# Attention and channel mixing on one core: a planned order of operations replaced by an order read from a table

## Chip, cores and metric

One core of a Trainium2 chip. The metric is the device time of one execution in microseconds (us). Engines: PE (matrix products, with PEld for its weight loads), DVE (vector engine), ACT (scalar engine), POOL (GpSimd), and SP, whose queue issues the DMAs.

## What is computed

Four batches, 8 heads, 768 tokens, head size 64, all in fp32. Attention is local, with 24 block summaries beside the near keys:

```python
k_sum = k.reshape(B, H, nb, 32, D).max(axis=3)
v_sum = v.reshape(B, H, nb, 32, D).mean(axis=3)
mask_l = np.abs(pos[:, None] - pos[None, :]) < 16
scores_s = scale * (q · k_sum) + np.log(32)
a = softmax(concat(where(mask_l, scale * q @ k.T, -1e9), scores_s))   # divided by sum + 1e-9
x = a @ concat(v, v_sum)                     # heads side by side: (4, 768, 512)
xk = mu_k * x + (1 - mu_k) * x_prev          # x_prev: the token before
xr = mu_r * x + (1 - mu_r) * x_prev
out = sigmoid(xr @ w_r) * (maximum(xk @ w_k, 0)**2 @ w_v)   # 512 -> 1024 -> 512
```

## The kernel before

**Tiling.** Two heads make a pair (128 partitions), 768 tokens two halves of 384. A *unit* is one batch, pair and half, 32 in all. For each: a score product (24 narrow products into two PSUM tiles, L511); per head and window of 128 rows a masked minimum on DVE (L525) and an exp on ACT that also sums (L529), six of each; epsilon added to the six sums (ACT, L533) and the reciprocal (DVE, L535); six multiplications by it, one per head and window of 128x120 (POOL L540 or ACT L545); two transposes on PE (L557), each copied out by ACT (L564); the values product (24 narrow products, L577), copied out by DVE (L591) or ACT (L593). There is one PSUM tile for transposes, one for values, two for scores, and four shared by all wide products.

**Wide work per batch and half.** Tokens are mixed with their predecessors (L651/L654 and L658), split into a rounded and a remaining part (L661 and L663; in one case on PE by diagonal matrices made at L314: L680, L684, L686). Each product then takes three terms: gate products (L703 to L705, 128x512), then a sigmoid (L719); expert products in eight steps *j*, a first one (L735, 12 of 128x384), its relu, square, cast and remainder (L740, L742, L744/L745, L746), and a second one (L757, L783). Three results per half are multiplied (L789) and stored (L793).

**Weights** come as 64-bit words and are put together before use: scaling (ACT L346, POOL L349), signs (L354), two joins on DVE (L358, L362), a cast (ACT L371, POOL L373) and the remainder (DVE L385). Keys are reduced to block maxima (L437 to L445) and copied between the keys (L449); in batch 0 the block means of v are made on PE (L461, L469) and spread to the windows (L475, DVE or POOL); in later batches they come from a transposed v (L406) and small DMAs.

**The order.** No loop order is kept: every operation becomes an `Op` with its engine, buffers, length (`LENGTH`) and alternatives on other engines. `schedule` counts due times backwards from fixed ones (`GATES`, `PERIOD`, `STEP`), shifted per group by `NUDGE`, and plays a list scheduler forwards; the sequence that it finds is the sequence in which instructions are emitted, for each engine's queue and for SP's DMAs. From batch 1 on, `chain` ties PE work of three units into one operation:

```python
parts.append(units[i].scores())
parts.append(units[i - 2].values())
parts.append(units[i - 1].turn(0))          # first transpose
group({1: "score", 2: "scoreT", 3: "chain"}[len(parts)] ..., min(due), *parts)
```

Until the first gate product, PE is kept at work with products of a zero tile (`still`, L849), as many as fit into the planned gaps.

Of the kernel before, what the change touches and what calls it, by code (L numbers as in the profile page):

```python
# [18 lines left out]
DM, DF = 512, 1024  # L19
# [18 lines left out]

LENGTH = dict(
    score=865, transpose=335, vtrans=200, vpool=900, vsel=240, spread=560, spread_p=830, values=1040, scoreT=1130, chain=1975, valuesT=1290, mixe=1400, minus=200, diag=290, wminus=1250, wevac=520, none=0, gate=2790, gate_p=2100, e1=2110,  # L40
    e2a=1400, e2b=700, e2=700, e2h=350, resulth=340,
    kred=860, kred2=460, kmax=90, kcopy=225, vred=865, mask=203, rc=110, evac=470, mixd=530, sub=472, psub=480, khv=276,
    result=605, wsign=575, eps=110, wor=605, wsub=605, tiny=60, wsign_d=335,
    exp=378, pts=362, vm=165, mixa=512, cast=405, relu=375, square=413, sigmoid=494, wscale=562, wcast=510,
    norm=340, norm_d=191, norm_a=285, mixa_d=329, wscale_p=575, wcast_p=575, mixa_p=575, kcopy_p=400, evac_a=362,
)
PORT = ("wor", "wsub", "mixd", "sub", "khv", "kcopy", "spread", "wsign_d", "norm_d", "mixa_d")
TAIL = dict(PE=60, DVE=85, ACT=100, POOL=30, SP=0)
LATENCY = dict(PE=230, DVE=130, ACT=150, POOL=150, SP=0)
DMA_NS_PER_BYTE = 1 / 390.0  # L50
DMA_FIXED = 2000
GATES = (36000, 62000)
PERIOD = 52000
STEP = 4800
SLACK = 400
WARM = 230
MIX_PE = ((0, 0, 1),)
SUB_PE = ()
TABLE = 1300

NUDGE = dict(
    chain10=-6500, chain11=47000, chain13=-2000, chain14=-3500, chain15=20500, chain16=8500, chain17=11500,
    chain18=-18500, chain19=17500, chain20=1500, chain21=26500, chain22=1500, chain23=-1000, chain24=-54000,
    chain25=-27000, chain26=10000, chain27=36500, chain28=-17500, chain30=1000, chain31=15500, chain32=-33000,
    chain33=-1500, chain35=-6000, chain36=6000, chain37=42500, chain38=26000, chain39=35000, e000=1500,
    e002=500, e003=2000, e004=2000, e005=-39500, e006=-27500, e007=9000, e010=-2500, e012=-7000, e013=-29000,
    e017=45000, e100=2500, e101=4500, e102=-60000, e103=-1000, e105=-500, e106=-5000, e107=60000, e110=-500,
    e112=-7000, e113=-1500, e116=-1000, e117=3000, e200=7500, e201=-26000, e202=4000, e204=500, e206=1000,
    e207=32500, e210=-60000, e211=-1500, e212=-9500, e213=-1000, e214=4500, e216=3500, e217=1500, e300=-46000,
    e301=-30500, e302=-23500, e303=500, e304=-1000, e306=2500, e307=1000, e310=-60000, e311=-34000, e312=-27000,  # L70
    e313=2000, e314=-1500, e316=-1000, e317=500, f000=-46500, f001=-5500, f003=-13500, f005=-10500, f006=22000,
    f007=20000, f010=3500, f011=18500, f012=-14000, f013=-14500, f014=-25500, f015=-8500, f016=-4000, f100=1500,
    f101=-2500, f103=-2500, f104=2500, f105=10000, f106=-3000, f107=19500, f110=6000, f111=9000, f112=20000,
    f113=13500, f114=-14500, f115=8500, f116=10000, f117=-500, f200=13000, f203=-500, f204=-8000, f205=-34000,
    f207=-12500, f211=-2000, f212=-9000, f213=-33500, f214=20500, f215=-3000, f216=10000, f217=-7000,
    f300=-24500, f302=-26000, f303=1500, f304=1500, f307=-9500, f310=-12000, f311=-19000, f312=2000, f313=-500,
    f314=-2500, f316=-500, gate00=9000, gate01=-3500, gate10=-60000, gate11=56000, gate20=16000, gate21=60000,
    gate30=2500, gate31=60000, means1=-24500, means2=-10500, mix000=-2000, mix001=3500, mix010=1000,
    mix011=14500, mix100=-10500, mix101=-32000, mix110=20500, mix111=-39500, mix200=-21500, mix201=-21500,
    mix210=8500, mix211=-32500, mix301=27500, mix310=11000, mix311=17000, set00=2000, set01=1500, set02=7000,  # L80
    set03=-41500, set10=-6000, set11=-7500, set12=2500, set20=-1500, set22=15000, set23=-10500, set31=-59500,
    set32=-44500, unit000=500, unit001=4000, unit010=1500, unit011=2000, unit020=-9500, unit021=17000,
    unit030=2500, unit031=-60000, unit100=-4000, unit101=-19500, unit111=-3500, unit120=-3500, unit121=-33000,
    unit130=-60000, unit131=-60000, unit200=-2500, unit201=1500, unit210=-18000, unit211=19000, unit220=-3000,
    unit221=26000, unit230=2000, unit231=4500, unit300=7000, unit301=-25500, unit310=-15000, unit311=-49500,
    unit320=-12000, unit321=-2000, unit330=4500, unit331=-10500, wk0=-8500, wk1=-7500, wk3=12500, wk4=-26500,
    wk5=-60000, wk6=-56000, wk7=-9500, wr0=500, wr1=-1500, wr3=-2500, wv0=2500, wv1=2000, wv2=-35500, wv4=-500,
    wv5=1500, wv6=-44000,
)
COLD = 10000  # L90
WR = 0, 6000
EARLY = 15000
FIRST = 5000
SECOND = 5000
UNITS = 6000
BETWEEN = 5, 6, 7
LOOSE = ("mm",)
NORM = ('ACT',)
MIXA = "POOL", "DVE"
FIRST_UNITS = [(hf, p) for hf in range(2) for p in range(NPAIR)]  # L100


class Buf:


    def __init__(self, pool, n):
        self.pool, self.n, self.users, self.left, self.t = pool, n, [], 0, None


class Op:  # L110
    def __init__(self, n, ways, due, bufs, size):
        self.n, self.ways, self.due, self.bufs, self.size = n, ways, due, bufs, size
        self.deps, self.succ, self.start, self.finish, self.eng = set(), [], None, None, None


class Plan:
    def __init__(self, pools):
        self.pools, self.ops, self.count = pools, [], {p: 0 for p in pools}
        self.writers, self.readers, self.tag = {}, {}, None
# [6 lines left out]
    def op(self, eng, cost, due, emit, reads=(), writes=(), size=0, other=None):  # L126

# [4 lines left out]
        ways, kinds = {eng: (LENGTH.get(cost, 0), emit)}, {eng: cost}  # L132
        for e, kind, way in ([other] if isinstance(other, tuple) else other or []):
            ways[e] = LENGTH[kind], way
            kinds[e] = kind
        o = Op(len(self.ops), ways, due, bufs, size)
        o.tag, o.kinds = self.tag, kinds
# [14 lines left out]
        o.name = cost  # L152
        return o

    def schedule(self):

        for o in self.ops:
            for d in o.deps:
                d.succ.append(o)
            for x in o.bufs:  # L160
                x.left += 1

        for o in reversed(self.ops):
            own = 1.0e9 if o.due is None else o.due
            wait = DMA_FIXED + o.size * DMA_NS_PER_BYTE if "SP" in o.ways else min(c for c, _ in o.ways.values()) + SLACK
            o.due = min([own] + [s.due - wait for s in o.succ])
        for o in self.ops:
            o.due += NUDGE.get(o.tag, 0)
        waiting = {o: len(o.deps) for o in self.ops}
        free_slots = {p: [(0, t) for t in ts] for p, ts in self.pools.items()}  # L170
        turn = {p: 0 for p in self.pools}
        table = None
        engines = {e: 0 for e in ("PE", "DVE", "ACT", "POOL", "SP")}
        ready = {e: [] for e in engines}
        dma = 0
        order = []
        port, holder = 0, None

        def locks(o, e):
            return e == "POOL" and o.kinds[e] not in ("tiny", "none") or e == "DVE" and o.kinds[e] in PORT  # L180

        def begin(o, e, at):
            at = max(at, engines[e])
            return max(at, port) if locks(o, e) and holder != e else at

        def released(o):
            for e in o.ways:
                at = max((d.finish + (0 if d.eng == e and e != "SP" else LATENCY[d.eng]) for d in o.deps), default=0)
                ready[e].append((o, at))

        for o in self.ops:
            if not waiting[o]:
                released(o)
        while any(ready.values()):
            best = None
            for e, now in engines.items():
                pick = None
                for o, at in ready[e]:
                    start, need, ok = max(at, now, o.due - EARLY if e == "SP" else 0), {}, True
                    for x in o.bufs:  # L200
# [7 lines left out]
                    if not ok:  # L208
                        continue
# [19 lines left out]
            if e == "PE" and start < COLD:  # L229
                o.cost *= 1.6  # L230
# [712 lines left out]
```

## Time and profile before

| | us |
|---|---|
| median of 3 runs (lowest, highest) | 455.13 (454.95, 456.5) |
| profiled execution | 454.91 |
| its span, first to last instruction | 453.1 |
| PE busy in the span | 444.6 (98%) |
| PEld | 379.4 (84%) |
| ACT | 304.3 (67%) |
| DVE | 273.4 (60%) |
| POOL | 59.2 (13%) |

The profiled execution's time holds 1.8 us outside its span. PE's clock is granted in full over the span as the profile's stages show it. "Busy" for PE counts modelled ends of pipelined products, so steps from start to start tell more of PE than its busy time.

### The profile page before, as it was taken

Reading aid. Unit: us, or ns where it says so; the run is one execution under the profiler, and the core shown is the slowest. Engines: PE = TensorE matmul, PEld = TensorE weight load, DVE = VectorE, ACT = ScalarE, POOL = GpSimd, SP = SyncE. Lnnn points to the kernel's source line nnn. Section 1 sums busy time; section 2 is a strip of 40 time slices with the busy share of each in tenths; the row PEclk is TensorE's granted clock in tenths of the full one; section 3 lists DMA queues with packets and bytes.
Section 4 is the critical chain, followed back from the end, with each engine's and each line's share of the span. In section 5 each row is a group of like instructions: output and inputs, shape, how many; then the busy total and the mean of one; then the engine's idle time right before and its main releaser. Section 6 shows DMA issues by size and latency. Waiting matters only on the chain.

```text
span 453.1 us, 9740 instructions
## 1 busy us (share of the span) xinstructions
PE 444.6 (98%) x3602; PEld 379.4 (84%) x3602; DVE 273.4 (60%) x876; ACT 304.3 (67%) x923; POOL 59.2 (13%) x137
## 2 busy tenths in 40 slices
PE   9998999999999999999999999999999999999996
PEld 8866788878988888888888788888888888889885
DVE  5999999997445696465345749474434473433212
ACT  3899999998986756786777735796767644332210
POOL 0472222202110110011111000110201000000000
PEclk9999999999999999999999999999999999999999
DMA  8973668846100074520700047632400010001001
GB/s 310 391 279 129 222 210 279 260 130 204 43 1 2 27 257 153 160 99 34 222 1 1 0 172 274 218 98 60 129 1 1 1 69 1 1 2 69 1 0 69
DMA packets 27446, 51.96 MB, mean 115 GB/s; under 512 B 2951, under 2 KB 15111, under 8 KB 27399
## 3 DMA queue, kind: packets, MB, share of 16 engines
q1 hardware_dynamic: 27399, 51.35, 33.5%
q8 instruction: 28, 0.46, 0.4%
q14 instruction: 19, 0.16, 0.1%
HBM read 43.28 MB, written 6.29 MB: 109 GB/s over the span
## 4 chain that ended last, share of the span: by engine, by line
PE 85%; ACT 6%; DVE 5%; issue 1%; DMA 1%; POOL 0%; DVEq 0%; POOLq 0%
PE mm L735 27%; PE mm L757 23%; PE av L577 5%; PE sc L511 5%; PE pt L557 5%; PE mm L703 4%; PE mm L704 4%; PE mm L705 4%; PE mm L783 3%; PE av L849 3%; ACT y L529 2%; ACT y L545 1%; DMA st<-in_w_k 1%; PE mm L680 1%; DVE wc L362 1%
## 5 line engine op out<-in xcount | busy, mean ns | idle before, releaser
L735 PE MATMUL mm<-xs,wk_h 128*128 128x384 f32 x512 | 101.2, 339 | 0.5 <-ACT r L740 0.3
L735 PEld LDWEIGHTS mm<-xs,wk_h 128*128 128x128 f32 x512 | 90.2, 188 | 5.7 <-ACT r L740 0.7
L529 ACT ACTIVATE y<-y,mn 128x120 f32<-128x120 f32 x192 | 73.5, 386 | 2.8 <-DVE mn L525 2.7
L740 ACT ACTIVATE r<-mm 128x384 f32<-128x384 f32 x64 | 30.8, 487 | 63.6 <-PE mm L735 55.6
L757 PE MATMUL mm<-wv_h,kh 128*128 128x512 f32 x168 | 68.1, 405 | 0.0
L757 PE MATMUL mm<-wv_l,kh 128*128 128x512 f32 x168 | 66.3, 395 | 0.0
L746 DVE TENSOR_TENSOR kl<-r,kh 128x384 fp32r<-128x384 f32 x64 | 35.7, 557 | 41.6 <-PE mm L757 38.0
L744 DVE CAST kh<-r 128x384 fp32r<-128x384 f32 x56 | 20.2, 361 | 62.5 <-PE mm L757 32.5
L540 POOL TENSOR_SCALAR y<-y,rc 128x120 f32<-128x120 f32 x81 | 30.7, 395 | 202.0 <-DVE rc L535 196.4
L735 PE MATMUL mm<-xs,wk_l 128*128 128x384 f32 x256 | 55.3, 337 | 0.0
L757 PE MATMUL mm<-wv_h,kl 128*128 128x512 f32 x168 | 50.4, 409 | 0.0
L525 DVE CUSTOM_DVE_ANT_0 y<-sc,mask_sb 128x120 f32<-128x120 f32 x192 | 42.1, 277 | 7.4 <-PE sc L511 7.3
L735 PEld LDWEIGHTS mm<-xs,wk_l 128*128 128x128 f32 x256 | 45.6, 188 | 0.0
L663 DVE TENSOR_TENSOR xs<-xa,xs 128x384 fp32r<-128x384 f32 x60 | 32.2, 557 | 15.6 <-ACT xs L661 15.5
L564 ACT COPY pts<-pt 120x384 f32<-120x384 f32 x64 | 30.3, 473 | 15.4 <-PE pt L557 14.7
L545 ACT ACTIVATE y<-y,rc 128x120 f32<-128x120 f32 x111 | 35.8, 387 | 5.2 <-DVE rc L535 4.7
L703 PE MATMUL mm<-wr_h,xs 128*128 128x512 f32 x96 | 38.7, 403 | 0.0
L705 PE MATMUL mm<-wr_h,xs 128*128 128x512 f32 x96 | 38.0, 395 | 0.0
L704 PE MATMUL mm<-wr_l,xs 128*128 128x512 f32 x96 | 38.0, 395 | 0.0
L658 DVE SCALAR_TENSOR_TENSOR xa<-vx,mu_sb,xa 128x384 f32<-128x384 f32 x60 | 36.3, 626 | 2.1 <-POOL xa L654 1.5
L757 PEld LDWEIGHTS mm<-wv_h,kh 128*128 128x128 f32 x168 | 31.6, 188 | 6.2 <-issue 0.2
L529 ACT ACTIVATION_READ_ACCUMULATOR y<-y,mn 128x1 f32 x192 | 36.5, 190 | 0.0
(81 smaller groups left out, 699.1 us busy)
## 6 DMA issues: line engine op xcount, KB each, us to landing
vx<-in_v SPq DMA_DIRECT2D x32, 384.0 KB
kt<-in_k SPq DMA_DIRECT2D x15, 544.0 KB
qt<-in_q SPq DMA_DIRECT2D x32, 192.0 KB
out<-z SPq DMA_DIRECT2D x23, 256.0 KB
st<-in_vT SPq DMA_DIRECT2D x12, 384.0 KB
st<-in_w_k SPq DMA_DIRECT2D x8, 512.0 KB
st<-in_w_v SPq DMA_DIRECT2D x8, 512.0 KB
st<-in_w_r SPq DMA_DIRECT2D x4, 512.0 KB
```

The source lines that it names most:

```text
L525: op("DVE", "mask", None, lambda h=h, i=i, var=var: nc.vector.tensor_tensor_reduce(out=y[h].t[:, i, :], in0=sc[h].t[:, i, 0:NK], in1=mask_ ...
L529: op("ACT", "exp", None, lambda h=h, i=i: nc.scalar.activation(y[h].t[:, i, :], y[h].t[:, i, :], AF.Exp, bias=mn[h].t[:, i:i + 1], scale=-1.0,
L545: nc.scalar.activation(y[h].t[:, i, :], y[h].t[:, i, :], AF.Copy, scale=rc.t[:, NSL * h + i:NSL * h + i + 1])
L658: op("DVE", "mixd", None, lambda xt=xt, xa=xa, p=p: nc.vector.scalar_tensor_tensor(out=xa.t, in0=xt.t[:, 1 + lo:1 + lo + HT], scalar=mu_sb ...
L663: op("DVE", "sub", None, lambda xa=xa, xh=xh, xl=xl: nc.vector.tensor_tensor(out=xl.t, in0=xa.t, in1=xh.t.bitcast(F32), op=ALU.subtract), ...
L703: nc.tensor.matmul(ps[i].t, xh.t[:, ts], wr_h[:, p, :], start=(p == 0), stop=False)
L704: nc.tensor.matmul(ps[i].t, xh.t[:, ts], wr_l[:, p, :], start=False, stop=False)
L705: nc.tensor.matmul(ps[i].t, xl.t[:, ts], wr_h[:, p, :], start=False, stop=(p == NPAIR - 1))
L735: nc.tensor.matmul(ps.t[:, 0:HT], w[:, j, p, :], x[p][s].t, start=(n == 0), stop=(n == 11))
L740: op("ACT", "relu", None, lambda: nc.scalar.activation(r.t, ps.t[:, 0:HT], AF.Relu), reads=[(ps, 0)], writes=[(r, 0)])
L746: op("DVE", "sub", None, lambda: nc.vector.tensor_tensor(out=kl.t, in0=r.t, in1=kh.t.bitcast(F32), op=ALU.subtract), reads=[(r, 0), (kh, 0 ...
L757: nc.tensor.matmul(acc[t].t, a.t[:, t * P:(t + 1) * P], w[:, j, :], start=start, stop=stop)
```

## The change

`schedule` no longer searches. It takes a table of the operations' numbers, in the order in which their calls stand in the code, and emits them in the table's sequence; a letter behind a number names the engine where it isn't the first one (D for DVE, A for ACT, P for POOL). Due times, `NUDGE` and the list scheduler are gone. What is left of the timing sets how many fill products are emitted and which buffer of a pool is taken, with new lengths, a price for changes between kinds of PE work, and latencies per kind.

```diff
-        while any(ready.values()):
-            best = None
-            for e, now in engines.items():
...
-                    key = (start if late else now, o.due, o.n)
...
+    def schedule(self, order):
...
+        for n, e in order:
+            o = self.ops[n]
+            o.eng = e = e or next(iter(o.ways))
+            k, o.emit = o.ways[e]
+            length = LENGTH.get(k, 0)
+            start = now[e]
+            if e == "PE":
+                start += SWITCH.get(kind + KINDS.get(k, "M"), 0)
+                kind = KINDS.get(k, "M")
+            for d in o.deps:
+                assert d.finish is not None, "an operation comes before one that it needs"
+                start = max(start, d.finish + (0 if d.eng == e and e != "SP" else d.latency()))
             for x in o.bufs:
                 if x.t is None:
-                    _, x.t = free_slots[x.pool].pop(0)
-                    turn[x.pool] += 1
...
+                    x.free, x.t = free[x.pool].pop(min(range(len(free[x.pool])), key=lambda i: free[x.pool][i][0]))
+                start = max(start, x.free)
...
-    order = plan.schedule()
+    order = plan.schedule([(int(x.rstrip("DAPS")), dict(D="DVE", A="ACT", P="POOL").get(x[-1])) for x in ORDER.split()])
```

`chain` and `group` go; `unit` makes one operation each of scores, first transpose, second transpose and values, for all batches. The normalisation becomes one operation per head, on DVE one instruction, on ACT or POOL three:

```diff
+        for h in range(2):
+            def norm(h=h):
+                nc.vector.tensor_tensor(
+                    out=y[h].t, in0=y[h].t, in1=rc.t[:, NSL * h:NSL * h + NSL].unsqueeze(2).broadcast_to([P, NSL, NK]),
+                    op=ALU.mult)
+
+            def norm_act(h=h):
+                for i in range(NSL):
+                    nc.scalar.activation(
+                        y[h].t[:, i, :], y[h].t[:, i, :], AF.Copy, scale=rc.t[:, NSL * h + i:NSL * h + i + 1])
...
+            op("ACT", "norm3_a", norm_act, reads=[*rows, (rc, 0)], writes=rows,
+               other=[x for x in (("DVE", "norm3", norm), ("POOL", "norm3_p", norm_pool)) if x[0] in NORM])
...
+        op("PE", "values", values, reads=[(vw, x) for x in "ab"] + [(pts[0], 0), (pts[1], 0)], writes=[(av, 0)])
```

In the table 22 of the 64 normalisations stand on DVE, 23 on ACT and 19 on POOL. Further operations get an alternative on DVE: the scaling and cast of weights, diagonals, epsilon, the copy of a transpose, relu, and the cast of mixed tokens. The buffers of a cast and remainder are numbered after the square, not before the product. The unused `minus_sb` goes. Gate products of the second half of batch 0 are no longer placed between fixed expert steps. The arithmetic is otherwise the same.

The table has 1938 numbers. 0 to 13 are constants and diagonals; 14 to 95 the weights w_r and the sets of keys and values of batch 0; 96 to 207 the weights w_k and w_v; from 208 the units of batch 0 (24 or 25 numbers each: query load, scores, six masks and exps, epsilon, reciprocal, two normalisations, two transposes with their copies, values, copy out); 404 to 415 the mixes on PE, 416 to 419 the first gate products, 423 on the next mixes, 439 and 444 the first two first expert products. Its beginning:

```diff
+ORDER = """
+21 22 1 14 208 4 0 2 25 26 27 28 5 43 3 56 233 36 24 23 256 29P 16 209 6 15 12D 13 11 17 210 218 214 216 215 9 44 45
+18 19D 220 212 10 8 63 219 211 217 213 221 46 47 258 231 58 83 48 49 57 222 20 234 283 76 65 64 59 38 239 308 243 223
+225D 224P 237 245 7 37 244 228 96 85 84 30 241 39 60 235 40 246 229 238 31 32 226 242 240 33 236 247 50 34 227D 248
+250D 230 61 249 41 51 35 66 251 52 67 68 69 42 259 53 252 232A 423 86 266 87 262 253 332 404 54 281 55 254 267 264 265
+88 260 89P 268 270 263 424 284 62 255 77P 269 405 261 271 285 293 291 295 294 78 70 272 287 289 257A 290 273 274D 309
+71 275D 79 296 72 276 356 103 110 407 427 97 286 73 80 277D 98 645 622 288 292 74 278 90 312 406 279 320 318 297D 75
+319 280 314 316 298 310 91 408 300 306 299D 99 92 333 93 425 301 100 105D 426 416 821 613 124 671 94 282 315 321 313
+409 342 112 344 302 101 317 410 303 106 311 102 322D 428 323 325D 345 343 431 417 104P 81P 411 429 304 338 340 324 341
+339 117 336 412 334 337 305 113 432 82 107 675 357 307A 326 435 335 436 346D 126D 413 111 108 1173 380 131 114 418 414
+430 433 119 415 347 109 115 327 437 349 328 127 419 125D 329 152 438 116 348 118 330 120 434 128 129D 138 350 444 121
...
```

## Rows read from the trace of the kernel before

**Rows 1.** Busy time of each engine in three stretches of the span: stretch, its us, busy us and instructions of PE, PEld, DVE, ACT and POOL, then PEclk, DMA share and GB/s.

```profile
0.00:54.15 54.15, 50.54 (x594) 40.29 (x594) 47.65 (x152) 43.03 (x155) 18.52 (x37) 1.00 0.73 265
54.15:103.50 49.35, 48.23 (x402) 39.97 (x399) 48.70 (x137) 47.05 (x137) 10.68 (x18) 1.00 0.69 221
103.50:453.10 349.60, 345.80 (x2612) 299.11 (x2610) 177.10 (x589) 214.23 (x633) 29.96 (x83) 1.00 0.23 76
```

**Rows 2.** Timeline of PE, first 57 us: start us, us, instructions merged where they follow one another.

```profile
0.99 8.76 PE L849 MATMUL av<-still 128*128 128x128 f32 x52 [0.99 <-POOL still L843]
...
35.66 0.48 PE L703 MATMUL mm<-wr_h,xs 128*128 128x512 f32 x1
...
54.15 1.66 PE L735 MATMUL mm<-xs,wk_h 128*128 128x384 f32 x8
```

**Rows 3.** The chain of waits from 30 to 60 us: start us, us, what the end waited for.

```profile
35.64 0.72 ACT y L545 x3
...
54.68 1.28 ACT L719
55.98 0.61 ACT z L719
```

**Rows 4.** Groups of DVE instructions from 0 to 54.15 us: out<-in, shapes, count, busy us, mean ns of one, idle time before them.

```profile
L358 DVE SCALAR_TENSOR_TENSOR we<-st,we 128x512 uint32<-128x512 uint32 x10 | 6.8, 690 | 0.1
...
L354 DVE TENSOR_SCALAR we<-st 128x512 f32<-128x512 f32 x8 | 4.8, 616 | 5.1 <-DMA st<-in_w_r 4.7 <-DMA st<-in_w_k 0.4
...
L475 DVE COPY vx<-vm 24x768 f32<-24x768 f32 x6 | 3.3, 569 | 0.1
...
L385 DVE TENSOR_TENSOR wk_l<-wc,wk_h 128x512 fp32r<-128x512 f32 x3 | 2.0, 682 | 0.0
L385 DVE TENSOR_TENSOR wv_l<-wc,wv_h 128x512 fp32r<-128x512 f32 x2 | 1.8, 920 | 0.0
L449 DVE COPY kt<-ks 128x288 f32<-128x288 f32 x3 | 1.4, 453 | 0.1
L535 DVE RECIPROCAL rc<-sm 128x6 f32<-128x6 f32 x6 | 1.1, 180 | 0.0
...
L591 DVE COPY vx<-av 128x384 f32<-128x384 f32 x1 | 0.5, 547 | 0.0
```

**Rows 5.** Groups of ACT instructions from 0 to 54.15 us, columns as in Rows 4.

```profile
L545 ACT ACTIVATE y<-y,rc 128x120 f32<-128x120 f32 x24 | 7.7, 387 | 0.8 <-DVE rc L535 0.8
...
L564 ACT COPY pts<-pt 120x384 f32<-120x384 f32 x10 | 4.7, 472 | 0.8 <-PE pt L557 0.8
...
L593 ACT COPY vx<-av 128x384 f32<-128x384 f32 x4 | 1.9, 475 | 0.0
...
L314 ACT ACTIVATE diag_sb<-ident_sb,om_sb 128x128 f32<-128x128 f32 x4 | 1.6, 401 | 0.0
...
L371 ACT CAST wv_h<-wc 128x512 fp32r<-128x512 f32 x2 | 1.3, 632 | 0.0
...
L533 ACT ACTIVATE sm<-sm 128x6 f32<-128x6 f32 x6 | 1.2, 208 | 0.0
...
L651 ACT ACTIVATE xa<-vx,om_sb 128x384 f32<-128x384 f32 x1 | 0.6, 617 | 0.0
```

**Rows 6.** Groups of DVE and of ACT over the whole span, columns as in Rows 4.

```profile
L746 DVE TENSOR_TENSOR kl<-r,kh 128x384 fp32r<-128x384 f32 x64 | 35.7, 557 | 41.6 <-PE mm L757 38.0 <-PE pt L409 2.8
...
L744 DVE CAST kh<-r 128x384 fp32r<-128x384 f32 x56 | 20.2, 361 | 62.5 <-PE mm L757 32.5 <-ACT r L742 29.6
...
L719 ACT ACT_TABLE_LOAD x8 | 10.3, 1283 | 0.1
...
L529 ACT ACT_TABLE_LOAD x7 | 9.0, 1283 | 0.1
```

**Rows 7.** Timeline of PE at changes between its kinds of work (start us, us): L577 values, L557 transposes, L511 scores, L735, L703 and L783 wide products.

```profile
52.90 0.54 PE L557 MATMUL pt<-ident_sb,y 128*120 128x128 f32 x3
53.37 0.85 PE L511 MATMUL sc<-kt,qt 64*64 64x120 f32 x24
...
100.96 0.40 PE L783 MATMUL mm<-wv_h,kl 128*128 128x512 f32 x1
101.28 0.84 PE L511 MATMUL sc<-kt,qt 64*64 64x120 f32 x24
...
102.91 0.54 PE L557 MATMUL pt<-ident_sb,y 128*120 128x128 f32 x3
103.21 0.48 PE L703 MATMUL mm<-wr_h,xs 128*128 128x512 f32 x1
...
361.98 0.48 PE L783 MATMUL mm<-wv_h,kh 128*128 128x512 f32 x1
362.30 0.39 PE L783 MATMUL mm<-wv_l,kh 128*128 128x512 f32 x1
362.53 0.39 PE L783 MATMUL mm<-wv_h,kl 128*128 128x512 f32 x1
```

**Rows 8.** Timeline of all engines around one copy of a transpose (start us, us).

```profile
94.43 0.54 PE L557 MATMUL pt<-ident_sb,y 128*120 128x128 f32 x3
...
95.40 0.47 ACT L564 COPY pts<-pt 120x384 f32<-120x384 f32 x1
...
95.92 0.54 PE L557 MATMUL pt<-ident_sb,y 128*120 128x128 f32 x3 [0.25 <-ACT pts L564]
```

More of the change, by code (lines that the diff above doesn't have):

```diff
@@ L53 @@
[L53 to L55 removed]
+    score=776, transpose=245, vtrans=82, vpool=800, vsel=75, values=848, mixe=1400, gate=2780, gate_p=2085, e1=2085,
+    e2a=1390, e2b=695, e2=695, e2h=350,
+    kred=860, kred2=460, kmax=130, kcopy=225, vred=865, mask=203, eps_d=75, rc=110, norm3=440, evac=470, pts_d=440,
+    mixd=530, mixa_d=329, sub=472, psub=472, khv=276, spread=575, wsign_d=340, wor=605, wsub=605, wscale_d=340, wcast_d=340,
+    diag_d=135, relu_d=470, result=605, resulth=340,
+    exp=379, eps=110, norm3_a=857, pts=362, vm=165, evac_a=362, mixa=512, cast=405, relu=375, square=425, sigmoid=494,
@@ L131, in op @@
                 bufs.append(x)
[L132 to L137, printed above, removed]
+        ways = {eng: (kind, emit)}
+        for e, k, way in [other] if isinstance(other, tuple) and other else other:
+            ways[e] = k, way
+        o = Op(len(self.ops), ways, bufs, size)
+        o.tag, o.name = self.tag, kind
         for x in reads:
@@ new lines, in schedule @@
+        free = {p: [(0, t) for t in ts] for p, ts in self.pools.items()}
+        now = dict(PE=0, DVE=0, ACT=0, POOL=0, SP=DMA_FIRST)
+        dma, table, kind, shared, holder = 0, None, "M", 0, None
+        out = []
+        for n, e in order:
[10 more added lines that the diff above has]
+                start = max(start, d.finish + (0 if d.eng == e and e != "SP" else d.latency()))
@@ L595, in group @@
-    def group(name, due, *parts):
-        emits = [x for x, _, _ in parts]
-        op("PE", name, due, lambda: [x() for x in emits],
-           reads=[r for _, rs, _ in parts for r in rs], writes=[w for _, _, ws in parts for w in ws])
-    def unit(*args):
-        u = Unit(*args)
-        group("score", u.due - 10000, u.scores())
-        u.soften()
-        for h in range(2):
-            group("transpose", u.due - 3500 + 800 * h, u.turn(h))
-            u.copy(h)
-        group("values", u.due - 1000, u.values())
-        u.keep()
@@ new lines, in unit, with kept, batch @@
+        if hf == 0:
+            xt = xts[b, p] = buf("vx")
+            op("POOL", "tiny", lambda: nc.gpsimd.memset(xt.t[:, 0:1], 0.0), writes=[(xt, "z")])
+        xt = xts[b, p]
+        def kept():
+            return xt.t[:, 1 + hf * HT:1 + (hf + 1) * HT]
+        op("DVE", "evac", lambda: nc.vector.tensor_copy(out=kept(), in_=av.t[:, 0:HT]), reads=[(av, 0)], writes=[(xt, hf)],
+           other=("ACT", "evac_a", lambda: nc.scalar.copy(out=kept(), in_=av.t[:, 0:HT])))
+    def batch(b):
+        means = block_means(b)
+        for p in range(NPAIR):
+            e = load_set(b, p, means)
+            for hf in range(2):
+                unit(b, p, hf, e)
```

638 lines of the change are left out of this document (263 added, 375 removed).

## Prediction, made before the changed kernel was run

> **What bounds the kernel now.** I read three views in this order: busy time by stage, PE's timeline for the points at which stages begin, then the chain of waits inside the first stage. I cut the stages at PE's first expert product (54.15 us) and its first one of the second half (103.5) [rows 1, 2]. From 103.5 on PE is busy 345.8 of 349.6 us, and the rest is the tail behind its last product; between the cuts it is busy 48.23 of 49.35. So no other engine can shorten these two stages by more than 1.1 us; only PE's own list can. Before 54.15 it is different. The reader should see that PE's 50.54 busy us there are padded: the run of 52 fill products at 0.99 is the first of 116, and real gate products start at 35.66 [rows 2]. DVE is busy 47.65 of 54.15 us there, ACT 43.03, the DMA engines 73% [rows 1]. The chain of waits runs over DVE until 35.6 and from there over ACT up to the table load at 54.68 [rows 3]. So the first stage is set by DVE and ACT together, and everything behind 54.15 is a solid PE list that starts when that stage ends. A gain must come from an earlier end of the first stage, from cheaper changes between kinds of PE work, or from stalls that go.
>
> **The first stage, step by step.** I numbered the operation calls of the changed kernel in code order and read the table up to its first expert product (444). Ahead of it PE has 7 scores, 5 values, 11 transposes, 4 pooled means with their 4 selections, 4 mixes and 4 gate products. PE's timeline of before shows exactly these counts ahead of 54.15. The same PE work is thus due at this point, and what lies ahead of it on DVE and ACT can be compared by counts.
>
> DVE loses 6 sign operations (8 to 2) at 0.616, 3 of its 20 joins at 0.690, all 6 spreads at 0.569, 2 subtractions of weights at 0.682 and a key copy at 0.453: 3.70 + 2.07 + 3.41 + 1.36 + 0.45 = 10.99 us [rows 4]. One mix copy goes and one diagonal and one small maximum come; I set them against each other. It gains 6 one-step normalisations, 2 copies of transposes at 0.547, 3 additions of the epsilon at 0.180 (priced as the reciprocal of the same tile), 2 weight casts and one scaling at 0.616. No cast of 512 columns stands in the trace; the 384-column cast takes 0.361, so 0.48 [rows 6].
>
> The one-step normalisation is not in the trace either: 128x360, two operands from SBUF, one of them broadcast. The nearest row with two such operands is the subtraction of 384 columns, 0.557, so 0.557 x 360/384 = 0.52 [rows 6]; I take this because the shape and the operand count are the same. The cheap bound is the broadcast copy of 288 columns at 0.453, the dear one a two-input instruction that met POOL's work, 0.920 [rows 4]. Added: 6 x 0.52 + 1.09 + 0.54 + 0.96 + 0.62 = 6.3. Net for DVE: 4.7 us less.
>
> What this row shows is that a second SBUF operand costs time: 0.557 against 0.361 for one operand at equal width [rows 6]. The Trainium skill (VectorE: DVE Perf Modes, "Why `tensor_tensor` can't do 2×_2P or 4×") says that the second tensor takes the read port that a one-input instruction uses to double its rate; this speaks against normalising by a two-tensor instruction, and the trace agrees. By that page's clock of 0.96 GHz and one column per cycle the step would be an estimated 0.375, and DVE's net 5.6 instead of 4.7.
>
> ACT: normalisations fall from 24 instructions to 5 x 3 = 15, 9 x 0.387 = 3.48; 2 transpose copies fewer 0.94, 3 epsilons 0.62, one value copy 0.48, one weight cast 0.63, one diagonal 0.40; 3 mix copies come, 1.85 [rows 5]. Net 4.7 us less. POOL takes the spreads and signs and gives up most normalisations and mix copies; it is busy 18.52 of 54.15, so this costs nothing as long as DVE and ACT remain the bound [rows 1]; if POOL's turn came late, the second values product of the first units would wait for its spread.
>
> SP's queue is reordered too: constants move between the first key, query and weight loads, and the first key loads keep the front. At 73% use the DMA engines have slack over the stage; a set of value windows that comes late would hold its pooled means on PE and the scores behind them. I put this at zero, covered by that slack.
>
> Both limiting lists shrink by 4.7 us. DVE was idle 54.15 − 47.65 = 6.5 us, of which 4.7 waiting for the first weights [rows 1, 4]. I keep this idle time. So PE's first expert product comes **4.7 us earlier**, at 49.4.
>
> **Changes between kinds of PE work.** Entering a score or values from a wide product costs 0.32 instead of a step of 0.23 (100.96 to 101.28), and so does the first wide product behind a transpose (361.98 to 362.30), 0.09 each. A score directly behind a transpose starts 0.47 after it (52.90), a wide product 0.30 after it (102.91), so this direct neighbourhood costs 0.17 [rows 7]. From the first expert product on, before has 34 entries from wide products, 56 returns from transposes and 8 from the narrow products: 98 x 0.09 = 8.8 us. The table has 15, 42 and 3, and 14 scores or values directly behind a transpose: 60 x 0.09 + 14 x 0.17 = 7.8. Untying thus does not add changes here; it **saves 1.0 us**, all on PE and so on the path.
>
> **What is taken as zero.** Two more table loads (17 changes between exp and sigmoid against 15) are 2 x 1.28 us of ACT [rows 6], both behind 103.5, where ACT has 135 us of idle time [rows 1]. The second expert product still needs an accumulator that the first sigmoid frees, and that sigmoid stands behind a table load. In the table 3.4 us of PE work lie between the last gate product and it, against 1.28 + 0.6 on ACT. The 1.1 us of stalls between the cuts I leave as they are: the lists are as full as before, DVE 48.70 of 49.35.
>
> **Sum.** −4.7 − 1.0 = −5.7 against the profiled execution's own 454.91: **449.2 us**. That execution lies 0.22 below the median of the runs shown, within their spread. About 0.5% (2.3 us) is what a measurement of this kernel can tell from no change.
>
> **Rivals.**
>
> A, the first stage also closes up. DVE's removable idle, 6.5 − 4.7 = 1.8, goes too, with the 1.1 of stalls between the cuts, and the normalisation costs 0.453 (6 x 0.07 = 0.4). Then 454.91 − 5.7 − 3.3 = 445.9. For it: before, DVE idles between 4 and 20 us and is full from there. Against: the idle time there is waiting for loads and for the first scores, which stay.
>
> B, the freed time turns into waits. Each engine now follows one fixed list; an operand that is late holds all that is queued behind it, and the first stage ends at 54.15 as before. Place: the copy of a transpose between PE and ACT. In the trace one took from 94.43 to 95.92, 1.49 us from transpose to transpose, because ACT was still casting [rows 8]. At 8 units behind the first expert product the table leaves only a score, 0.95 us, between the second transpose (0.25) and its values, so such a delay stalls PE 0.29 each, 2.3 us; similar waits ahead of it would eat the rest. Only the changes of kind remain: 453.9. Against: ACT is less full than before.
>
> C, slower. The broadcast operand makes DVE take the one-step normalisation as three passes, 3 x 0.557 = 1.67 each. Its place is the stretch in which DVE is the bound; 8 of the 22 on DVE lie before 103.5. They would add 8 x 1.15 = 9.2 to DVE's list: 449.2 + 9.2 = 458.4. It is slower than before by what can be told from (5.7 + 2.3)/8 = 1.0 more each, from 1.52 on. Against: the broadcast copy of 288 columns takes 0.453, no pass per block [rows 4].
>
> Milder than C, and inside my own case: the two-input normalisation may collide with POOL. The subtraction takes 0.920 for one set of weights and 0.682 for another [rows 4]. At 0.92 each the six add 2.4 us, 451.6. The Trainium skill (GPSIMD Engine Reference, "1. Specifications") says that POOL shares its SBUF interfaces with VectorE and that instructions with two SBUF inputs contend; the spread of these rows fits that, without showing it.
>
> **Chances.** My case 0.52, A 0.22, B 0.16, C 0.10. My case and A are faster by over 0.5%: 0.74. B is the same: 0.16. C is slower: 0.10. The range runs from 444.0 to 454.5. The low end is 1.9 below A, what eight collisions would give back at 0.920 − 0.682 = 0.238 each, since the rows that I count with include them. The high end takes in B with 0.6 to spare. Below it I leave a small part of A, above it C.
>
> **What would show it.** In the changed profile: the first expert product near 49.4; DVE busy near 43.0 and ACT near 38.3 ahead of it; 22 two-input normalisations of 128x360 at about 0.52; the span from the first expert product to the last product about 1.0 shorter than before. The prediction is wrong in its main step if the first expert product comes after 52 although DVE's list is shorter: then waits between engines, not the length of the lists, set the first stage. It is wrong in the second if PE shows more than 2 us of waits behind it. A normalisation of 1.5 us or more is C.

## The result, and the profile after

The change makes the kernel slower: **460.67 us** median (458.49 to 461.91) against 455.46 for the kernel before beside it, ratio 1.0098, 95% interval 1.0069 to 1.0127. The forecast was 449.2, and its range ended at 454.5. The profiled execution after took 458.49 us (before: 454.91), at the same granted clock, 1.00. It is the fastest of that kernel's nine executions, so the traces show 3.6 us of a loss that is 4.5 by the ratio.

The stages of after, cut at PE's first expert product and 98.2 us (answers to [rows 1]; columns as there):

```profile
core 0: us, PE busy (x) PEld busy (x) DVE busy (x) ACT busy (x) POOL busy (x), PEclk, DMA share, GB/s
0.00:51.70 51.70, 47.88 (x584) 37.76 (x584) 43.90 (x148) 40.96 (x141) 18.50 (x32) 1.00 0.82 290
51.70:98.20 46.50, 43.86 (x315) 36.78 (x313) 44.94 (x115) 41.43 (x108) 10.49 (x16) 1.00 0.59 197
98.20:456.70 358.50, 351.55 (x2698) 304.66 (x2696) 211.52 (x680) 188.49 (x561) 45.94 (x96) 1.00 0.25 78
```

PE's timeline after: fills, first score, first expert product (answers to [rows 2]; start us, us):

```profile
0.99 6.99 PE L751 MATMUL av<-still 128*128 128x128 f32 x48 [0.99 <-POOL vx L545]
7.91 0.84 PE L474 MATMUL sc<-kt,qt 64*64 64x120 f32 x24
...
51.70 1.63 PE L653 MATMUL mm<-xs,wk_h 128*128 128x384 f32 x8
```

The first expert product comes 2.45 us earlier (54.15 to 51.70), but from there to the end of the last product PE needs 400.97 us instead of 395.15, with the same products. DVE's waits ahead of it, before and then after, and its groups before 51.7 (answers to [rows 4]):

```profile
DVE we L354 <- DMA st<-in_w_r: 4.7, 2, 4.2
...
DVE we L354 <- DMA st<-in_w_k: 0.4, 1, 0.4
```

```profile
DVE kg L410 <- DMA kt<-in_k: 3.6, 2, 3.5
DVE diag_sb L296 <- DMA ident_sb<-in_ident: 2.6, 1, 2.6
```

```profile
...
L334 DVE SCALAR_TENSOR_TENSOR we<-st,we 128x512 uint32<-128x512 uint32 x9 | 6.1, 680 | 0.0
L338 DVE SCALAR_TENSOR_TENSOR wc<-wc,we 128x512 uint32<-128x512 uint32 x8 | 5.5, 684 | 0.4 <-ACT wc L323 0.3
L410 DVE TENSOR_REDUCE kg<-kt 128x48 f32<-128x768 f32 (+1 forms) x5 | 3.9, 788 | 3.6 <-DMA kt<-in_k 3.6
L499 DVE TENSOR_TENSOR y<-y,rc 128x360 f32<-128x360 f32 x6 | 3.9, 662 | 0.1
L359 DVE TENSOR_TENSOR wr_l<-wc,wr_h 128x512 fp32r<-128x512 f32 x4 | 3.7, 922 | 0.0
```

The one-step normalisation over the whole run (duration ns min/median/max), then PE's waits behind the first expert product, and of DVE's there those for key loads (us in total, times, longest us):

```profile
L499 DVE TENSOR_TENSOR y<-y,rc x22: 521/532/1093, 15.3 to 357.9; 128x360 f32<-128x360 f32 x22
```

```profile
PE mm L678 <- DVE kh L666: 1.3, 1, 1.3
PE sc L474 <- DVE mn L484: 1.2, 1, 1.2
PE mm L653 <- DVE r L661: 0.8, 1, 0.8
PE pt L522 <- DVE y L499: 0.7, 1, 0.7
PE mm L678 <- DVE kl L668: 0.6, 1, 0.6
PE mm L624 <- ACT z L638: 0.5, 1, 0.5
```

```profile
...
DVE kg L410 <- DMA kt<-in_k: 9.4, 4, 3.9
...
DVE kg L414 <- DMA kt<-in_k: 2.1, 1, 2.1
...
```

Two rows more of this view are waits for loads, 1.2 us together. Before, DVE waits for no load there, and PE's view is this:

```profile
PE pt L557 <- ACT pts L564: 0.6, 2, 0.4
PE mm L735 <- ACT r L740: 0.3, 1, 0.3
```

After, PE waits for DVE, and DVE for loads. How the one becomes the other is plain at 180 us. The chain of waits, then DVE's timeline and PE's:

```profile
167.65 6.33 DMA vx<-in_v
174.04 0.82 SPq L455
174.91 4.47 DMA kt<-in_k
179.58 0.52 DVE xa L577
```

```profile
179.41 0.17 DVE L414 TENSOR_REDUCE kg<-kt 128x1 f32<-128x16 f32 x1 [2.10 <-DMA kt<-in_k]
179.49 0.61 DVE L577 SCALAR_TENSOR_TENSOR xa<-vx,mu_sb,xa 128x384 f32<-128x384 f32 x1
...
181.27 0.36 DVE L666 CAST kh<-r 128x384 fp32r<-128x384 f32 x1 [0.97 <-ACT r L663]
```

```profile
181.68 0.50 PE L678 MATMUL mm<-wv_h,kh 128*128 128x512 f32 x1 [1.32 <-DVE kh L666]
```

SP's spread of block means (L455) overwrites rows of a value load and waits for it; the key load stands behind that in SP's fixed queue, the key maximum behind the key load in DVE's, a mix, a mask and the cast behind the maximum (ACT's exp, relu and square between mask and cast), and PE behind the cast.

### The profile page after: what moved, and what is told of

Its sections match the earlier page's. It is cut to its first block, busy times and chain, and to the rows that moved or that the text cites. A ratio compares the mean times of both kernels' runs of the same rounds, so it can differ in the third digit from the quotient of the medians.

```text
span 456.7 us, 9661 instructions
## 1 busy us (share of the span) xinstructions
PE 443.3 (97%) x3592; PEld 379.2 (83%) x3592; DVE 300.4 (66%) x941; ACT 270.9 (59%) x809; POOL 74.9 (16%) x143
## 4 chain that ended last, share of the span: by engine, by line
PE 71%; DVE 14%; DMA 7%; ACT 4%; issue 2%; SPq 1%; DVEq 0%; ACTq 0%
PE mm L653 24%; PE mm L678 23%; PE av L537 4%; PE pt L522 4%; PE mm L626 3%; PE mm L624 3%; PE mm L625 3%; PE sc L474 3%; DMA kt<-in_k 3%; PE mm L704 3%; DVE y L484 2%; DVE xa L577 2%; DMA vx<-in_v 1%; DVE we L334 1%; DVE wc L338 1%
## 5 line engine op out<-in xcount | busy, mean ns | idle before, releaser
L663 ACT ACTIVATE r<-r 128x384 f32<-128x384 f32 x64 | 33.2, 522 | 47.0 <-DVE r L661 46.2
L484 DVE CUSTOM_DVE_ANT_0 y<-sc,mask_sb 128x120 f32<-128x120 f32 x192 | 47.4, 275 | 10.0 <-PE sc L474 7.9
L678 PE MATMUL mm<-wv_h,kl 128*128 128x512 f32 x168 | 48.9, 399 | 0.6 <-DVE kl L668 0.6
L577 DVE SCALAR_TENSOR_TENSOR xa<-vx,mu_sb,xa 128x384 f32<-128x384 f32 x60 | 38.5, 648 | 5.3 <-POOL xa L573 4.5
L510 POOL TENSOR_SCALAR y<-y,rc 128x120 f32<-128x120 f32 x57 | 25.3, 460 | 98.4 <-DVE rc L496 79.8
L659 ACT ACTIVATE r<-mm 128x384 f32<-128x384 f32 x37 | 18.0, 488 | 36.8 <-PE mm L653 30.2
L678 PEld LDWEIGHTS mm<-wv_h,kl 128*128 128x128 f32 x168 | 30.8, 188 | 7.4 <-DVE kl L668 1.2
L678 PEld LDWEIGHTS mm<-wv_l,kh 128*128 128x128 f32 x168 | 31.6, 188 | 6.2 <-DVE wv_l L359 0.3
```

Of the source, the lines that this page charges most:

```text
L484: op("DVE", "mask", lambda h=h, i=i, var=var: nc.vector.tensor_tensor_reduce(out=y[h].t[:, i, :], in0=sc[h].t[:, i, 0:NK], in1=mask_sb[:, ...
L510: nc.gpsimd.tensor_scalar(out=y[h].t[:, i, :], in0=y[h].t[:, i, :], scalar1=rc.t[:, NSL * h + i:NSL * h + i + 1], scalar2=1.0, op0=ALU.mul ...
L577: op("DVE", "mixd", lambda xt=xt, xa=xa, p=p: nc.vector.scalar_tensor_tensor(out=xa.t, in0=xt.t[:, 1 + lo:1 + lo + HT], scalar=mu_sb[:, wh ...
L663: op("ACT", "square", lambda: nc.scalar.activation(r.t, r.t, AF.Square), reads=[(r, 0)], writes=[(r, 0)])
L678: nc.tensor.matmul(acc[t].t, a.t[:, t * P:(t + 1) * P], w[:, j, :], start=start, stop=stop)
```

## The experiments

One table first. "To the end" runs from the first expert product to the end of the last product. Ratios are to the kernel before on the same chip. In e1's profiled execution the granted clock was 0.50 for 10.2 us, so its stages are not read. In e7, its e9 and e10 one transpose of a unit more stands behind that point, some 0.3 us of the third column.

| | first score | first expert product | to the end | ratio (95%) |
|---|---|---|---|---|
| before | 9.68 | 54.15 | 395.15 | 1 |
| after | 7.91 | 51.70 | 400.97 | 1.0098 |
| e1 POOL cut | – | – | – | 0.9979 (0.9954 to 1.0004) |
| e2 more buffers | 9.44 | 52.68 | 400.64 | 1.0085 (1.0053 to 1.0117) |
| e3 both | 8.33 | 49.57 | 398.16 | 0.9946 (0.9928 to 0.9963) |
| e4 table with slack | 9.34 | 54.73 | 399.90 | 1.0100 (1.0068 to 1.0131) |
| e5 keys untied | 8.84 | 52.21 | 397.94 | 1.0049 (1.0028 to 1.0070) |
| e6 keys and POOL | 9.02 | 50.24 | 397.24 | 0.9927 (0.9905 to 0.9948) |
| e8 three-step norm | 9.23 | 53.24 | 402.99 | 1.0182 (1.0125 to 1.0240) |
| e7 second table | 8.99 | 52.32 | 399.52 | 1.0010 (0.9981 to 1.0039) |
| e7b its sibling | 10.83 | 52.71 | 398.60 | 1.0009 (0.9984 to 1.0034) |
| e9 after, fewer fills | 7.63 | 51.72 | 403.81 | 1.0168 (1.0108 to 1.0229) |
| e9 e7, fewer fills | 6.79 | 50.62 | 398.91 | 0.9980 (0.9962 to 0.9999) |
| e10 third table | 8.56 | 51.45 | 396.60 | 0.9951 (0.9931 to 0.9970) |

**e1, POOL's passes cut.** Every POOL pass but seven on a few columns, as here:

```
-                        out=y[h].t[:, i, :], in0=y[h].t[:, i, :],
+                        out=y[h].t[:, i, 0:8], in0=y[h].t[:, i, 0:8],
```

> The kernel after, with POOL's passes cut to 8 columns (signs, mixing, normalisation) or one window (block copies, spreads); this leaves out most of those results, and only seven passes that scale or cast weights stay whole. Table, order and every other engine's work are the same. Theory A (the table has no slack, so late loads and passes stretched beside POOL both go through to PE): POOL's part is some 5 us, nearly 3 of it before PE's first expert product, which comes near 49 instead of 51.7; the last product near 447.5, ratio to before about 0.999. Rival B (POOL beside DVE alone is the loss): stalls behind the first expert product back at 2 to 3 us, ratio at most 0.987. Rival C (late loads alone): no change, ratio 1.008 to 1.012.

454.63 us: 1.2% or 5.4 us less than after, as theory A had it; rivals B and C fall. The stage split comes from e3 and e6. There the first expert product is 3.1 and 2.0 us earlier than in e2 and e5, and 1.1 and −0.2 of that is an earlier first score: POOL's part of the first stage is 2.0 to 2.2 us (nearly 3 was expected). The run does not tell two things apart: passes of DVE and POOL that hold each other up, and POOL's own passes, whose results now come sooner (128x120 in 0.27 us for 0.37). Nor was POOL cut in the kernel before, where it has passes beside DVE's too; so 5.4 us is the price of POOL's work in this table, not what the change added.

**e2, one more buffer for loads.**

```
-        kt=tiles("kt", 4, ...), qt=tiles("qt", 3, ...), ...
+        kt=tiles("kt", 5, ...), qt=tiles("qt", 4, ...), ...
...
-        st=tiles("st", 3, ...), ...
+        st=tiles("st", 4, ...), ...
```

> The kernel after with one more buffer each for staged loads (st 3 to 4), keys (kt 4 to 5) and queries (qt 3 to 4), so that loads that wait for a buffer are issued earlier; room comes from not keeping the low part of w_r, in whose place the gate multiplies the high part twice (a part of the result is left out, the number of products is the same). Table and order are the same. Theory A: the first expert product stays near 51.7, the stalls behind it shrink by 3.5 to 5.5 us, ratio to before near 1.000. Rival B (POOL beside DVE alone): no change, 1.008 to 1.012. Rival C (late loads alone): 9 us less, ratio near 0.990.

A miss: 0.1% less, within the interval. DVE's waits for keys behind the first expert product fall from 11.5 to 5.2 us, and PE's time there by 0.3: what a wait on DVE costs is what PE has queued behind it. The one at 177 us stays, since a buffer was not what the load stood for:

```profile
172.84 0.82 SPq L454 DMA_DIRECT2D vx<-vm  x1
173.76 0.46 SPq L399 DMA_DIRECT2D vx<-in_v  x1
174.78 0.81 SPq L454 DMA_DIRECT2D vx<-vm  x1
175.69 0.47 SPq L395 DMA_DIRECT2D kt<-in_k  x1
```

The key load goes out behind two spreads that wait for value loads, in the table's order, buffer or not.

**e3, both.**

> Both edits of the two runs before this one together (most of POOL's work and the low part of w_r left out). Theory A: the two parts add up to 8.5 to 10.5 us, ratio to before 0.987 to 0.991, and PE's time in stalls behind the first expert product is near that of the kernel before, some 2 us. Where one of the rivals holds, this run is no faster than the better of the two.

452.65 us, 0.9946: 6.9 us less than after by the ratios, a miss of the 8.5 to 10.5 expected, as e2 already was.

**e4, a table with slack for loads.** Order and engines searched again (262 operations change engine) on these constants, and the exclusion of DVE and POOL left out (`SHARED = ()`), because lengths were taken as they ran (the kernel after keeps the two apart by whole operations in its reckoning):

```
-    ... norm3=440, ...
...
-    ... norm3_p=1020, ...
+    ... norm3=499, ... norm3_p=1301, ...
...
-DMA_FIRST, DMA_ISSUE, DMA_START, DMA_END, DMA_BYTES_PER_NS = 740, 470, 700, 1350, 380.0
+DMA_FIRST, DMA_ISSUE, DMA_START, DMA_END, DMA_BYTES_PER_NS = 740, 475, 1150, 1800, 380.0
```

> The kernel after with another table, the whole computation kept: searched from the old table, with lengths as the run after has them (POOL's normalisation 1301 ns for 1020, DVE's 499 for 440, first expert products 2130 for 2085), loads that land 0.9 us later, and the sum taken over four sets of lengths and delays, some of them later still. By that reckoning the old table ends its last product at 446 to 454 (452.7 in the trace) and the new one at 438 in all four. Theory A: the last product at 440 to 446, ratio to before 0.975 to 0.988. Rival D (the losses come with the new structure or the one-step normalisation whatever the order): ratio 1.005 or more.

A miss, and the most useful one. DVE has no wait for a load behind 52 us any more, and still nothing is won: passes of POOL and DVE now stretch where they meet. DVE's joins before 54.7 us take 810 and 894 ns (680 and 684 in after), and POOL's normalisation before 110 us has ten times the passes (30 for 3), more than half of them over 0.45 us where the median in after is 0.37:

```profile
L328 DVE SCALAR_TENSOR_TENSOR we<-st,we 128x512 uint32<-128x512 uint32 x9 | 7.3, 810 | 0.2 <-POOL we L324 0.2
L332 DVE SCALAR_TENSOR_TENSOR wc<-wc,we 128x512 uint32<-128x512 uint32 x8 | 7.1, 894 | 0.4
```

```profile
L504 POOL TENSOR_SCALAR y<-y,rc 128x120 f32<-128x120 f32 x30 | 21.5, 731 | 3.2 <-DVE rc L490 3.1
```

So late loads and passes that collide are two losses, and a table has to hold both.

**e5, DVE freed of key loads.**

```
-                in_=blocks()[:, lo:hi, 0:QW].rearrange(...
+                in_=read()[:, lo:hi, 0:QW].rearrange(...      # b > 0: wr_h, resident
```

> The kernel after, but from batch 1 on DVE's maxima over the key blocks read resident weights in place of the loaded keys, and their copies go to a spare tile (the true block keys of batches 1 to 3 are left out). So nothing on DVE waits for a key load behind the first batch; PE's scores still do. Theory A, made sharper by the trace of after: DVE waits 3.0 us at 107.4, 1.6 at 124.0 and 2.1 at 177.3 for keys that land late, and PE's operands stand behind it in DVE's fixed queue; PE's stalls at 112 to 114 (1.9 us), 129 (0.35), 142 (0.45) and 181.7 (1.5) go, 4.2 us together, first expert product unchanged near 51.7, ratio to before 0.998 to 1.003. Rival: PE's scores wait for the same loads anyway and the stalls only change their name: ratio 1.007 or more.

2.2 us less than after by the ratios (give or take 1.6), 3.0 less behind the first expert product in the traces; the stalls at 112 to 142 us go, the one at 181.7 halves. Theory A in kind, 1 to 2 us short in size. The waits view of PE has lost its row for scores behind masks:

```profile
PE mm L659 <- DVE r L667: 0.8, 1, 0.8
PE pt L528 <- DVE y L505: 0.7, 1, 0.7
PE mm L684 <- DVE kh L672: 0.6, 1, 0.6
PE mm L630 <- ACT z L644: 0.5, 1, 0.5
PE mm L684 <- DVE kl L674: 0.5, 1, 0.5
```

**e6, e1 and e5 together.**

> The edit of e5 and POOL's cut passes of e1 together (block keys of batches 1 to 3 and most of POOL's results left out). Theory A: the two parts are different stalls and add up: 5.2 us (measured in e1) and 4.2, so some 9.4 less than after, ratio to before 0.986 to 0.992; stalls of PE behind the first expert product at most 3 us, the first expert product at 49.5 to 50.1. This is about where the forecast stood, and the account of its error would be closed. If something else holds back more than 2 us, ratio 0.994 or more.

451.9 us, 7.8 less than after by the ratios; the parts, 5.4 and 2.2, add up; the ratio is just outside the expected band, the first expert product too (50.24). What is left to the forecast is 2.4 us (454.91 x 0.9927 = 451.6 against 449.2), and two stalls near 173 and 177 us hold that much: there DVE waits 2.6 us for a transposed value load.

**e8, the one-step normalisation undone on DVE.**

```
-                nc.vector.tensor_tensor(out=y[h].t, in0=y[h].t, in1=rc...broadcast_to([P, NSL, NK]), op=ALU.mult)
+                for i in range(NSL):
+                    nc.vector.tensor_scalar(out=y[h].t[:, i, :], in0=y[h].t[:, i, :], scalar1=rc..., ...)
```

> The kernel after with the one-step normalisation undone where the table puts it on DVE: 22 normalisations as three passes with a scalar per partition each, at the same places of the queue. If the one-step form was the loss (it costs what three passes do, or more beside POOL): no change or faster, ratio 1.004 to 1.010. By the trace (451 ns back to back, 575 ns mean busy in one step; three passes are each about 190 to 210 ns and half of one's fixed cost more): 0.1 to 0.2 us more each, at most 1.5 us on the path, ratio 1.009 to 1.014.

Slower than after, by 3.8 us by the ratios, which one of the four executions (467.28) drives, by 1.7 by the medians; PE's time behind the first expert product is 2.0 longer. The expected band ended at 1.014, inside this interval. From first start to last end the three passes take 747 ns on the mean, the one 575, so 22 x 0.17 = 3.8 us of DVE: how much of it shows, half or all, these runs do not settle. The one-step form is not the loss; rival C is out.

**e7, a table with both losses.** The exclusion, kept instruction by instruction in the search, and late loads (214 operations change engine, POOL's fall from 100 to 84); and a sibling of it.

> The whole computation, the kernel after with a table searched again, this time with both losses in the reckoning: an operation of POOL and one of DVE that share a port keep each other out instruction by instruction in the order in which they ask, and loads land as the runs have them (270 bytes per ns in the first 8 us, then 395, and 0.5 to 1.4 us later than the old table had it). By this reckoning the old table's last product ends at 445, 451 and 454 in three settings (452.7 in the trace of after), e4's, which had left the port out, at 462 to 464 (454.6 in its trace), and the new one's at 440 to 441. Theory A: the last product at 440 to 445, ratio to before 0.975 to 0.988, no wait of DVE for a key load over 1 us behind 52 us. Rival D (the losses come with the structure whatever the order): ratio 1.003 or more.

> A second table from the same reckoning by another search, which starts PE's first expert product 2.9 us later by plan (50.1 for 47.1) and ends its last product at the same 440.5. If what counts is the whole plan and not the first stage alone: the same ratio as the first table within 0.005. If an early first expert product counts by itself: 2 to 3 us slower than the first.

Both 0.9% better than after and level with before, far from the 440 to 445 of the reckoning: a miss in size. That the table (order and choice of engines) was the loss and not the structure is shown, here against after and by e10 against the kernel before; that two tables with first expert products planned 2.9 us apart come out equal tells little, since in the traces they are 0.4 apart.

**e9, fewer fills ahead of the first score.** In e7's trace the first score starts only when the fills end. The edit, then fills and first score of e7, then the same with 14 fills (28 instructions):

```
-            for _ in range(int((o.start - end) // WARM)):
+            for _ in range(int((o.start - end) // (WARM if end > 600 else 400))):
```

```profile
0.99 8.06 PE L744 MATMUL av<-still 128*128 128x128 f32 x48 [0.99 <-POOL still L738]
8.99 0.44 PE L467 MATMUL sc<-kt,qt 64*64 64x120 f32 x8
```

```profile
0.99 5.87 PE L744 MATMUL av<-still 128*128 128x128 f32 x28 [0.99 <-POOL still L738]
6.79 0.85 PE L467 MATMUL sc<-kt,qt 64*64 64x120 f32 x24
```

> The table of e7 with 14 instead of 24 fill products ahead of the first score, the whole computation kept. In e7's trace the fills end at 9.05 and the first score starts at 8.99, while the last packets of its query are in at 5.9, so that it could start near 7.2. If the first stage hangs on that score: 1.5 to 1.9 us faster than e7, ratio to before 0.996 to 0.998. If DVE's list and not the first score sets the stage: less than 0.5 us, ratio 1.000 to 1.002.

> The whole computation, the kernel after with 13 instead of 24 fill products ahead of PE's first score. In the profiles so far the fills run at a step of 213 ns until PE's clock rises, which came at 3.9 us in after but at 4.8 to 7.1 in the other runs, and at 112 ns from then on; so the same 48 instructions end at 7.9 in after and up to 9.1 in others, while the first score's query has landed by 7.9. If the fills hold the first score back in most executions: 0.3 to 0.8 us faster than after, ratio to before 1.006 to 1.010. If they do not, or the clock falls in the gap that opens: 1.010 or more.

In e7 the stage moves with the score: score 2.20 us earlier, first expert product 1.70, ratio 0.998. In after it does not: the score then waits 1.29 us for its query, the stage ends as before, and the run is slower for two other reasons. One is the clock, which the expectation had named: three of the four executions had a mean granted clock of 0.993 to 0.996 and took 463.1 to 466.9 us, the profiled one, at 1.00, 461.3. The other is in the trace, 2.8 us behind the first expert product. The same key load as above took 6.1 us from issue to use (176.32 to 182.40) where it took 4.5, and PE's stall behind it doubled, from 1.3 to 2.7 us. DVE's wait for it:

```profile
182.40 0.17 DVE L414 TENSOR_REDUCE kg<-kt 128x1 f32<-128x16 f32 x1 [3.53 <-DMA kt<-in_k]
```

Why it landed later there stays open; with this table nothing absorbs it.

**e10, a third table**, from e7's, with the fewer fills (e7's constants in the kernel; 87 operations on POOL).

> The whole computation, a third table, with the fewer fills. Searched from e7's two tables on lengths raised to what their traces show (4% more on DVE and 12% on POOL for passes that share a port, 30 ns more between engines, one pass in ten up to half longer, first score not before 7.5). By that reckoning e7's table ends its last product at 445 to 448 and this one at 442 to 443. If the reckoning now has the losses in it: 3 to 5 us faster than e7, ratio to before 0.989 to 0.995. If a search on any reckoning mainly finds what that reckoning has wrong: ratio 0.997 or more.

453.8 us, 0.9951 (0.9931 to 0.9970): faster than both kernels, just outside the near edge of the expected band. Against e9 on e7, which has the fewer fills too, PE needs 2.3 us less to the end, but the first expert product comes 0.8 later: the first score now waits 1.8 us for its query. PE's waits behind 52 us, the whole answer; DVE has none there for a load:

```profile
PE mm L672 <- DVE kl L662: 0.8, 1, 0.8
PE sc L468 <- DVE mn L478: 0.4, 1, 0.4
PE mm L647 <- ACT r L653: 0.3, 1, 0.3
```

## Why the prediction was wrong

Between the forecast and the profiled execution lie 9.3 us (458.49 − 449.2): 2.25 in the first stage and 6.8 behind it. The step that failed most is that everything behind 54.15 is "a solid PE list that starts when that stage ends", with its stalls left "as they are": PE's stalls there, nearly all of them waits for DVE, grew by some 5 us.

**First stage, −4.7 forecast, −2.45 measured.** The direction and, but for one weight cast, the counts held: DVE's busy time fell 3.75 us (4.7), ACT's 2.07, or 2.5 without the part of a table load that now lies ahead of the cut (4.7). Some of the difference is price: the row means overlap where instructions follow one another (two normalisations of 0.39 take 0.68 on ACT, at 49.76), and busy time counts the overlap once. Two steps failed. One is that POOL's share "costs nothing as long as DVE and ACT remain the bound". POOL's busy time did not grow, but passes beside it stretch: the normalisation took 0.662 in this stage for 0.52, the subtraction of w_r 0.922 for 0.68 (that of w_v 0.640, for 0.920 before). e3 and e6 price POOL's work here at 2.0 to 2.2 us; how much of that the change added is not shown. The milder case beside rival C had the mechanism and put 2.4 us on it. The other is SP's new order, put at zero: the idle time kept at 6.5 was 7.8, and 6.2 of it are waits for other loads than before, keys and the identity (views above). So rival A, which took some of the idle time away, falls too.

And −2.45 is in part luck. In after's profile the fills sped up at 3.9 us, before at 6.7, and the first score came 1.8 us earlier. In e2, e5 and e8, whose table is the same (e8 normalises in three passes), the fills sped up at 7.1, 5.8 and 6.7, and the first expert product came at 52.68, 52.21 and 53.24, 0.9 to 1.9 us earlier than before; the prediction's sign for its main step, a first expert product after 52, would have stood there.

**Changes between kinds, −1.0 forecast.** By the steps between products it is −0.75: right.

**Stalls left as they are, 0 forecast.** Here the sign was lost: the stretch behind the first expert product became 5.8 us longer instead of 1.0 shorter. Single stalls over 0.13 us beyond the usual step add up to 2.0 us before and 7.1 after; the rest, some 1.5 us, lies in shorter delays. The prediction's own sign for this, over 2 us of PE waits there, is in the view above (5.1). Rival B had the mechanism, an operand late in a fixed queue, but at the wrong place (the copy of a transpose) and with a floor at "same as before". e5 shows that DVE's key maxima are some 2 to 3 us of it. POOL's work has a part in the stalls between 60 and 92 us, which fall from 3.1 us (e5) to 1.1 (e6) without it; but in e6 the two near 173 and 177 grow, and PE's time to the end is only 0.7 shorter (2.5 in e3 against e2). What POOL's work costs behind the first expert product lies by these traces between 0.7 and 2.5 us, and that it costs more than in the kernel before is not shown by a run; the rows speak for it (POOL's normalisation takes 460 ns on the mean, 395 before).

**SP's order, zero, by the DMA engines' 73% share.** The share was the wrong row to read. Behind 98.2 us the DMA engines are busy 25%, and DVE waits for keys there; in the chain at 180 us what counts is what stands ahead of one load in SP's queue and how much earlier than its use it is issued. The kernel before may issue up to 15 us ahead of a due time (its constant `EARLY`) and shows no such wait; that this is the reason was not tried.

**The normalisation, 0.52 forecast.** Median 0.532, mean 0.575 us (19 of 22 within 0.54, three from 0.75 to 1.09): right, and e8 shows it to be no dearer than three passes, so C falls. One slip stands in the text: 103.5 us is not the first expert product of the second half in before, which comes at 109.14; no term of the sum hung on it.

The table's own plan says the same in one number. With its exact lengths it ends the last product at 435.5 us, and the trace at 452.7; the old planner, whose latencies and loads carry margins, says 442.6, and the trace 449.3. The plan became 7 us shorter and the chip 17 us late on it. What stays open: how much of the loss POOL's collisions add to those of the kernel before, the split of the last 2 us between transposed value loads and other waits, and why e10 still ends 5 us behind its reckoning (448.05 against 443).

## What to carry to other kernels

Before believing a searched order, look for what its model leaves no room for: read which operations stand directly behind a load or behind a pass that shares a port with another engine, and price each by what queues behind it, not by the busy share of the resource. A search finds the errors of its model first, as e4 did with the port, so run a table, put its worst waits into the model and search again; here the third round paid. An old planner's margins may be part of its speed, and one profiled execution may be a lucky one.

## What the runs showed of the hardware that was not expected

PE's fills at the start run at a step of 213 ns and then at 112, nearly the ratio of its two levels (1.2 and 2.4 GHz); PE had run nothing but fills. The view prints a granted clock of 1.00 there too, but the trace has no record of the clock ahead of the change: the first begins at 3.9 us in after and 6.7 before, so that "granted in full over the span" holds from there on. The change came anywhere from 3.91 us (after's profile) to 7.12 (e7b), so the same 48 instructions end between 8.0 us (after) and 9.5 (e2) and move the first score with them.

In e1's profiled execution the granted clock fell to 0.50, 1.2 GHz, at 111.0 us, behind a stall of PE of 1.9 us that had ended at 109.9, and at 182.7, inside one of 3.4 us; it was back at 1.00 after 3.4 and 6.8 us.

A DVE pass and a POOL pass that meet take turns: in e4 two joins, 0.68 us each as a rule in after, took 1.92 beside two POOL copies that took 2.50, where one takes 0.82 at best. The Trainium skill (SBUF — State Buffer, "SBUF: two separate sides") says that the port pair which the two engines share is an exclusive lock, held for a whole instruction, while the other engine blocks; these rows agree: one join stays at 0.69 us and the other takes 1.31, each copy 1.27 or more. A table reckoned without that rule was e4.

```profile
19.57 1.92 DVE L332 SCALAR_TENSOR_TENSOR wc<-wc,we 128x512 uint32<-128x512 uint32 x2
```

```profile
19.67 2.50 POOL L442 COPY vx<-vm 24x768 f32<-24x768 f32 x2 [0.75 <-POOL wc L320]
```

From 3 to 8 us the loads of after move 289 GB/s and those of before 378 at the same DMA share, 0.98 and 1.03; which load order makes the difference was not tried.
